# Casting k and q of the first pair inside the set-up of the decays, and loading f on the Activation queue

## The chip, the cores and the metric

The kernel runs on one core of a Trainium2 chip. The metric is the device time of one execution in microseconds (us), as the median of several runs.

## What is computed

Two blocks in a row. The first is causal attention with a forget gate over 8 batches, 8 heads, 576 positions and a head size of 64; the second mixes the sequence in the frequency domain with one 512 x 512 complex matrix for each of 64 modes. Cut to what matters:

```
scores = (q @ k.T) / 8
cum    = cumsum(log(clip(f, 1e-4, 1)))            # one row of 576 for each batch and head
attn   = softmax(causal(scores + cum[i] - cum[j]))
x      = (attn @ v), heads side by side           # 8 x 576 x 512
X      = rfft(x over the sequence)[:64 modes]
Y      = X @ (w_r + i w_i), mode by mode          # 2 x 64 x 512 x 512 weights, float32 in HBM
u      = x + irfft(Y)
out    = u + relu(u @ w_ch)
```

## The kernel before

The attention is worked through in 32 steps `s`, two for each of 16 pairs. A pair is two batches and two heads, and its two steps are the two heads. For each pair, k, q and v are loaded into staging tiles (`emit_loads`, lines 254 to 273). There are three sets of staging tiles, `STG = 3`, so pair 3 uses the tiles of pair 0 again. All loads except f and v of pair 0 are issued on the GpSimd queue (POOL in the profile) by `pool_dma`, and in the order in which they are written. Between them, on the same queue, stand the weight tiles of the modes (`emit_w_load`): each is two transfers of 512 KB into one of nine ring buffers `wb`.

`emit_transposes(pr, what)` (lines 474 to 517) brings one of k, q, v of a pair into the layout that the matmuls need. First VectorE (DVE) casts the staging tile into a tile `kb`, `qb` or `vb` (lines 482 and 486). For v this is a product with `wdec9`, a table of decays. Then TensorE (PE) transposes nine blocks in two groups of five and four (line 500), each group into one PSUM tile `tp`. Then each group is copied out: k by ScalarE (ACT) into `KT` (line 513), q by VectorE into `QTs` (line 515), v by ScalarE into `VT` (line 517). The pool `psT`, with the tag "tr", has two PSUM buffers. The set-up of the decays uses the same two buffers.

The set-up of the decays comes first. f is loaded, ScalarE takes its logarithm (line 344), VectorE sums it along the row (the scan, line 349) and makes two rearranged copies `cum2` (line 360). TensorE transposes the sums into `cum_ps` (line 353), with `ident_f`, the float32 copy of the identity (line 331), as one operand. VectorE copies them to `cumT`, TensorE broadcasts one row of that into `R_ps`, VectorE forms `biasA` and ScalarE its exponential `wdec` (line 389), of which VectorE then clears a corner (line 390). Then nine transposes of `cum2` go to two PSUM tiles `cum9_ps`, five and four (line 397); VectorE subtracts them from a constant (line 404, two instructions for each tile), and ScalarE's exponential of that is `wdec9` (line 412). Behind all this comes `emit_transposes(0, "kqv")`.

In each step the scores go through PSUM to ScalarE's exponential `E` (line 559), are masked by VectorE (line 574), and are multiplied with v (line 597). From step 9 on, matmuls of the modes (line 186) stand between them, and each mode tile that is done frees a ring buffer for the next weight load.

A scheduler orders each engine's instructions by the order in which they are written and by when it thinks that their inputs are ready. `tc.keep_in_program_order(ins)` pins an instruction behind the instruction that was written just before it for the same engine. Before the change, the casts of the first three pairs, the loads on the GpSimd queue and the three iotas of the set-up are pinned.

Of the kernel before, what the change touches and what calls it, by code (L numbers as in the profile page):

```python
# [9 lines left out]
BF16 = mybir.dt.bfloat16  # L10
I32 = mybir.dt.int32
ALU = mybir.AluOpType
# [3 lines left out]
def _strided(ap: bass.AP, free_dims, offset_elems: int = 0) -> bass.AP:  # L16
    new_ap = [list(ap.ap[0])] + [list(x) for x in free_dims]
    return bass.AP(tensor=ap.tensor, offset=ap.offset + offset_elems, ap=new_ap)
# [3 lines left out]
def kernel(  # L22
# [11 lines left out]
    nc = tc.nc  # L34
    B, H, S, Dh = q.shape
# [7 lines left out]
    NDC = D // 128  # L43
    BH = B * H
# [9 lines left out]
    RP = 64  # L54
    NR = S // RP
    RG = ((0, 5), (5, 4))
    NRING = 9
    STG = 3
# [9 lines left out]
    ident_bf = const.tile([128, 128], BF16, name="ident_bf")  # L68
    wch = const.tile([128, NDC, D], BF16, name="wch")
    bas = const.tile([128, NSB + 1, 2, NM], BF16, name="bas")  # L70
    sel = [const.tile([128, 130], BF16, name=f"sel{r}") for r in range(2)]
# [12 lines left out]
    def tile_of(n):  # L84
# [2 lines left out]
        g = (n - NTH + GL) % NTH  # L87
        return 2, g ^ 4 if GL // 2 <= g < GL else g

    def pool_dma(dst, src):  # L90
        tc.keep_in_program_order(nc.gpsimd.dma_start(dst, src))  # L91

    def wb_tile(n, *dims):
        if n != late.get("nx"):
# [111 lines left out]
    def stage(i):  # L206
        if i != 1:
            return {
                nm: stq.tile(
                    [128, 2, NR, Dh], F32 if nm == "v" else BF16, name=f"st{nm}{i}"  # L210
                )
                for nm in "kqv"
            }
        n = 2 * NR * Dh
        flat = {
            "k": wx[:, 0:n],
            "q": wx[:, n : 2 * n],
            "v": wx[:, 2 * n : 4 * n].bitcast(F32),
        }
        return {  # L220
            nm: t.rearrange("p (b r d) -> p b r d", b=2, r=NR)
            for nm, t in flat.items()
        }

    with ExitStack() as actx:
        stq = actx.enter_context(tc.tile_pool(name="stq", bufs=1))
        qkb = actx.enter_context(tc.tile_pool(name="qkb", bufs=2))
        kt = actx.enter_context(tc.tile_pool(name="kt", bufs=1))
        qtp = actx.enter_context(tc.tile_pool(name="qtp", bufs=2))
# [11 lines left out]
        psT = actx.enter_context(  # L241
            tc.tile_pool(name="psT", bufs=2, space=bass.MemoryType.PSUM)
        )
# [6 lines left out]
        wdec9 = ssb.tile([128, NR, B, NDC], BF16, name="wdec9")  # L250
        NE = 2
        QKVst = [stage(i) for i in range(STG)]
        VTs = [kt.tile([128, 2, SP], BF16, name=f"VT{i}") for i in range(2)]
        KTs = [kt.tile([128, 2, SP], BF16, name=f"KT{i}") for i in range(2)]
        Es = [epl.tile([128, 2, EW], BF16, name=f"E{i}") for i in range(NE)]

        steps = [(dc, bp, h) for dc in range(NDC) for bp in range(B // 2) for h in (0, 1)]
        NPR = len(steps) // 2

        def emit_loads(pr):  # L260
            dc, bp, _ = steps[2 * pr]
            for nm, src in (("k", k), ("q", q), ("v", v)):
# [9 lines left out]
                else:  # L272
                    pool_dma(dst, ap)

        used = [0]

        def scratch(parts, *dims):
# [11 lines left out]
        ident_f = scratch(128, 128)  # L289
        ftf = scratch(128, S)  # L290
        ft = ftf[:BH, :]
        nc.sync.dma_start(ft[:], f.rearrange("b h s -> (b h) s"))
        emit_loads(0)
        nc.gpsimd.memset(trimask[:, :], 1.0)
        nc.gpsimd.affine_select(
# [32 lines left out]
        tc.keep_in_program_order(  # L328
            nc.gpsimd.iota(m_i[:], pattern=[[1, NM]], base=0, channel_multiplier=0)
        )  # L330
        nc.vector.tensor_copy(ident_f[:, :], ident_bf[:, :])
        for r, t in enumerate(sel):
            nc.vector.memset(t[:, :], 0.0)
            nc.vector.tensor_copy(
                _strided(t[:, 1:2], [[2, 64]]), _strided(ident_bf[:, r : r + 1], [[2, 64]])
            )
        for t in VTs:
            nc.vector.memset(t[:, :, S:SP], 0.0)
        for t in KTs:
# [3 lines left out]
        lf = ft  # L343
        nc.scalar.activation(lf[:], ft[:], ACT.Ln)
        wide = scratch(128, 2 * S)
        onesS = wide[:BH, 0:S]
        nc.vector.memset(onesS[:], 1.0)
        cum = scratch(BH, S)
        nc.vector.tensor_tensor_scan(cum[:], onesS[:], lf[:], 0.0, ALU.mult, ALU.add)
        cum_ps = psT.tile([128, NSB, BH], F32, tag="tr", name="cum_ps")  # L350
        for sc in range(NSB):
            ns = SBLK[sc]
# [4 lines left out]
            )  # L357
        cum2 = wide[:BH, :].rearrange("c (r h p) -> c r h p", r=NR, h=2)
        for h in range(2):
            nc.vector.tensor_copy(  # L360
                cum2[:, :, h, :], _strided(cum[:, 0:1], [[1, NR], [NR, RP]])
            )
        cumT = scratch(128, NSB, BH)
        nc.vector.tensor_copy(cumT[:, 0:4, :], cum_ps[:, 0:4, :])
        nc.vector.tensor_copy(cumT[:64, 4, :], cum_ps[:64, 4, :])
        ones_row = scratch(1, 128)
        nc.vector.memset(ones_row[:], 1.0)
        R_ps = psT.tile([128, BH], F32, tag="tr", name="R_ps")
# [5 lines left out]
            stop=True,  # L374
        )
        Rb = ssb.tile([128, BH], F32, name="Rb")
        nc.vector.tensor_copy(Rb[:], R_ps[:])
        biasA = scratch(128, NSB, BH)
        nc.vector.tensor_tensor(
            biasA[:, 0:4, :],  # L380
            _strided(Rb[:, :], [[0, 4], [1, BH]]),
            cumT[:, 0:4, :],
            ALU.subtract,
        )
        nc.vector.tensor_tensor(
            biasA[:64, 4, :], Rb[:64, :], cumT[:64, 4, :], ALU.subtract
        )
        nc.vector.memset(biasA[64:128, 4, :], 0.0)
        nc.scalar.activation(wdec[:, :, :], biasA[:, :, :], ACT.Exp)
# [1 line left out]
        bias9 = ftf[:, 0 : NR * B * NDC].rearrange(  # L391
            "p (r b c) -> p r b c", r=NR, b=B
        )
        for r0, n in RG:
            cum9_ps = psT.tile([128, 5, BH], F32, tag="tr", name="cum9_ps")
            for r in range(r0, r0 + n):
                nc.tensor.transpose(
                    cum9_ps[:, r - r0, :],
                    cum2[:, r, :, :].rearrange("c h p -> c (h p)"),
                    ident_f[:BH, :BH],  # L400
                )
            for h in range(2):
                hs = slice(h * 64, h * 64 + 64)
                nc.vector.tensor_tensor(
                    bias9[hs, r0 : r0 + n, :, :],
                    _strided(Rb[hs, h : h + 1], [[0, n], [H, B], [2, NDC]]),
                    _strided(
                        cum9_ps[hs, 0, h : h + 1], [[BH, n], [H, B], [2, NDC]]
                    ),
                    ALU.subtract,  # L410
                )
        nc.scalar.activation(wdec9[:, :, :, :], bias9[:, :, :, :], ACT.Exp)

# [54 lines left out]
                    BI[:, sc * 128 : (sc + 1) * 128], bip[:, :], coef[:], None, ALU.mult  # L468
                )


        QT, vaugs = {}, {}

        def emit_transposes(pr, what):
            dc, bp, _ = steps[2 * pr]
            for which in what:
                st = QKVst[pr % STG][which]
                if which == "q":
                    QT[pr] = qtp.tile([128, 2, S], BF16, tag="QT", name="QTs")
                sb = qkb.tile([128, NR, 2, Dh], BF16, tag="cb", name=which + "b")  # L480
                if which != "v":
                    ins = nc.vector.tensor_copy(
                        sb[:, :, :, :].rearrange("p r b d -> p b r d"), st[:, :, :, :]
                    )
                else:
                    ins = nc.vector.tensor_tensor(
                        sb[:, :, :, :],
                        st[:, :, :, :].rearrange("p b r d -> p r b d"),
                        _strided(
                            wdec9[:, 0, 2 * bp, dc : dc + 1],  # L490
                            [[B * NDC, NR], [NDC, 2], [0, Dh]],
                        ),
                        ALU.mult,
                    )
                if pr < STG:
                    tc.keep_in_program_order(ins)
                for r0, n in RG:
                    tp = psT.tile([128, 5, 2, RP], BF16, tag="tr", name="tp")
                    for r in range(r0, r0 + n):
                        nc.tensor.transpose(  # L500
                            tp[:, r - r0, :, :].rearrange("c h p -> c (h p)"),
                            sb[:, r, :, :].rearrange("p b d -> p (b d)"),
                            ident_bf[:, :],
                        )
                    tv = tp[:, 0:n, :, :].rearrange("c r h p -> c h p r")

                    def rows(t):
                        return t.rearrange("c h (p r) -> c h p r", r=NR)[
                            :, :, :, r0 : r0 + n
                        ]  # L510

                    if which == "k":
                        nc.scalar.copy(rows(KTs[pr % 2][:, :, 0:S]), tv)  # L513
                    elif which == "q":
                        nc.vector.tensor_copy(rows(QT[pr][:, :, :]), tv)  # L515
                    else:
                        nc.scalar.copy(rows(VTs[pr % 2][:, :, 0:S]), tv)  # L517

        def emit_vback(s):
            dc, bp, h = steps[s]  # L520
# [166 lines left out]
        def next_w():  # L687
            nonlocal nload
            if nload < NDC * NG:
                emit_w_load(nload)  # L690
                nload += 1

        emit_transposes(0, "kqv")
        for s in range(NS + 1):
            pr, h = s // 2, s % 2
            if s == 0:
# [10 lines left out]
            if pr + 1 < NPR:  # L707
                emit_transposes(pr + 1, ("kq", "v")[h])
# [24 lines left out]
    with ExitStack() as bctx:  # L733
# [80 lines left out]
        with ExitStack() as cctx:  # L814
            psBig = cctx.enter_context(
                tc.tile_pool(
                    name="psBig", bufs=6, space=bass.MemoryType.PSUM, side="right"
# [79 lines left out]
            while nmode < NT - 1:  # L897
# [9 lines left out]
                if nmode > NT - GL:  # L907
                    assert nx == B
                    while done < (nmode - NT + GL) * (len(parts) - 2) // (GL - 2):
                        a, sb = parts[done]  # L910
# [4 lines left out]
            for a, sb in parts[done:]:  # L915
# [5 lines left out]
                    name=name,  # L921
# [127 lines left out]
        for b in range(2, B):  # L1049
            for t in range(2):  # L1050
# [4 lines left out]
                name="psX", bufs=1, space=bass.MemoryType.PSUM, reuse_waits="tile"  # L1055
# [56 lines left out]
```

## Time and profile before

| | |
|---|---|
| median of 7 runs | 438.2 us (436.59 to 438.82) |
| the profiled execution's own time | 438.23 us |
| its span in the profile | 436.4 us |
| busy: PE, DVE, ACT, POOL | 83%, 60%, 52%, 29% of the span |
| bytes moved by DMA | 97.37 MB, mean 223 GB/s |
| landing of f after its issue | 2.9 us |
| landing of k, q, v of pair 0 after their issue | 6.6, 7.2, 5.4 us |

The span is the part of the execution that the profile covers; 1.8 us lie around it. "Idle before" in a row of the timeline is the time in which that engine had nothing to do before the row, with what ended the wait. A releaser is inferred, so where the named one had long been done, it was another one. A row of several instructions (x2, x9) carries the time from the start of the first to the end of the last, or their busy time where there are gaps.

### The profile page before, as it was taken

How to read it: one execution, taken by the hardware profiler on the slowest of the kernel's cores; microseconds unless marked ns; L12 is line 12 of the kernel's file. 1: busy time of each engine (PE TensorE's matmuls, PEld its weight loads, DVE VectorE, ACT ScalarE, POOL GpSimd, SP SyncE). 2: the span in 40 equal slices, each digit the busy share in tenths (PEclk: the TensorE clock that was granted, in tenths of full speed). 3: DMA queues.
4: the chain of work that ended last, by engine and by line, in shares of the span. 5: the costliest groups of instructions: out<-in, count | busy, mean ns of one | idle time of the engine just before them, and what ended most of it. 6: DMA issues, size and time to landing. Idle time of an engine off the chain costs nothing.

```text
span 436.4 us, 12194 instructions
## 1 busy us (share of the span) xinstructions
PE 363.1 (83%) x5247; PEld 248.7 (57%) x5265; DVE 263.0 (60%) x658; ACT 225.5 (52%) x340; POOL 128.7 (29%) x202
## 2 busy tenths in 40 slices
PE   2697699998978879788778988699999997799881
PEld 1464466776665656556656666566665654454440
DVE  5678778877455656545556578632332665544892
ACT  3678378775526264364553727124334443633770
POOL 7333332153233232332333221233222223200600
PEclk9997889998558686656585569689999999989997
DMA  8999999999999999999999999999999999995697
GB/s 179 234 235 241 234 236 239 231 197 238 228 220 237 219 229 236 211 237 228 219 237 212 210 212 211 211 210 212 211 212 211 211 211 212 211 211 104 239 370 281
DMA packets 50693, 97.37 MB, mean 223 GB/s; under 512 B 3760, under 2 KB 12944, under 8 KB 50640
## 3 DMA queue, kind: packets, MB, share of 16 engines
q0 software_dynamic: 46688, 86.16, 100.9%
q1 hardware_dynamic: 3632, 9.91, 6.3%
q8 instruction: 41, 0.67, 0.6%
q10 hardware_dynamic: 320, 0.52, 0.5%
q14 instruction: 12, 0.10, 0.1%
HBM read 163.73 MB, written 9.44 MB: 397 GB/s over the span
## 4 chain that ended last, share of the span: by engine, by line
PE 31%; DMA 28%; ACT 12%; DVE 9%; issue 4%; POOL 1%; ACTq 0%; DVEq 0%
DMA wb<-in_moe_w_i_dram 25%; ACT E L559 8%; PE pav L597 7%; PE ps L552 6%; PE A L186 5%; PE tp L500 5%; DMA stv<-in_v_dram 3%; DVE QTs L515 2%; PE px L640 2%; ACT KT L513 2%; PE vp L524 2%; DVE XT L654 1%; ACT VT L517 1%; DVE os L984 1%; PE px L665 1%
## 5 line engine op out<-in xcount | busy, mean ns | idle before, releaser
L559 ACT ACTIVATE E<-ps 128x1024 bf16<-128x1024 f32 (+1 forms) x128 | 101.6, 852 | 28.7 <-PE ps L552 19.1
L91 POOL DMA_DIRECT2D wb<-in_moe_w_r_dram x64 | 42.6, 665 | 132.9 <-PE A L186 38.5
L186 PE MATMUL A<-XT,wb 128*128 128x16 bf16 x1984 | 69.7, 181 | 10.0 <-DMA wb<-in_moe_w_i_dram 5.3
L186 PEld LDWEIGHTS <-wb 128*128 128x128 bf16 x1984 | 63.3, 100 | 24.7 <-issue 11.8
L552 PE MATMUL ps<-QTs,KT 64*128 64x64 bf16 (+4 forms) x384 | 58.6, 329 | 15.2 <-ACT E L559 14.0
L91 POOL DMA_DIRECT2D wb<-in_moe_w_i_dram x64 | 42.3, 660 | 73.7 <-DMA wb<-in_moe_w_i_dram 33.2
L597 PE MATMUL pav<-va,E 128*128 128x65 bf16 (+1 forms) x1088 | 58.3, 216 | 4.1 <-DVE x_all L619 3.5
L597 PEld LDWEIGHTS <-E 128*128 128x128 bf16 (+1 forms) x1088 | 48.0, 119 | 19.4 <-issue 8.4
L574 DVE TENSOR_TENSOR E<-E,trimask 128x256 bf16<-128x256 bf16 (+2 forms) x128 | 37.1, 302 | 19.5 <-ACT E L559 18.9
L517 ACT COPY VT<-tp 128x640 bf16<-128x640 bf16 (+1 forms) x32 | 23.3, 755 | 33.3 <-PE tp L500 33.0
L845 ACT CAST XW<-pxw 128x512 bf16<-128x512 f32 x36 | 20.7, 587 | 35.3 <-PE pxw L838 23.4
L552 PEld LDWEIGHTS <-KT 64*128 64x128 bf16 x384 | 19.2, 100 | 30.5 <-issue 21.8
L888 ACT CAST XW<-pB 128x512 bf16<-128x512 f32 x36 | 21.0, 586 | 28.2 <-PE pB L806 21.0
L838 PE MATMUL pxw<-wch,yy 128*128 128x512 bf16 x133 | 33.3, 382 | 1.1 <-issue 0.5
L887 DVE CAST x_all<-pA 128x512 bf16<-128x512 f32 x36 | 24.9, 692 | 15.4 <-PE pA L806 14.5
L513 ACT COPY KT<-tp 128x640 bf16<-128x640 bf16 (+1 forms) x32 | 22.1, 754 | 22.2 <-PE tp L500 22.2
L515 DVE COPY QTs<-tp 128x640 bf16<-128x640 bf16 (+1 forms) x32 | 23.2, 767 | 14.3 <-PE tp L500 14.2
L619 DVE TENSOR_TENSOR x_all<-pav,rcp 128x384 bf16<-128x384 f32 x64 | 29.1, 454 | 0.8
L608 DVE RECIPROCAL rcp<-pav 128x6 f32<-128x6 f32 x64 | 12.1, 189 | 27.5 <-PE pav L597 26.6
L151 DVE TENSOR_TENSOR YTe<-A,Yacc 128x128 bf16<-128x128 f32 x16 | 5.9, 368 | 32.8 <-PE A L186 32.8
L806 PEld LDWEIGHTS <-ident_bf 64*64 64x64 bf16 (+1 forms) x300 | 14.1, 107 | 16.5 <-issue 8.4
L524 PE MATMUL vp<-ident_bf,VT 128*128 128x128 bf16 x160 | 18.2, 259 | 5.0 <-DVE QTs L515 4.2
(143 smaller groups left out, 606.0 us busy)
## 6 DMA issues: line engine op xcount, KB each, us to landing
wb<-in_moe_w_r_dram POOLq DMA_DIRECT2D x62, 512.0 KB, 16.5
wb<-in_moe_w_i_dram POOLq DMA_DIRECT2D x62, 512.0 KB, 17.1
out_dram<-os SPq DMA_DIRECT2D x12, 512.0 KB, 5.2
stv<-in_v_dram POOLq DMA_DIRECT2D x10, 576.0 KB, 15.4
stk<-in_k_dram POOLq DMA_DIRECT2D x11, 288.0 KB, 15.3
stq<-in_q_dram POOLq DMA_DIRECT2D x11, 288.0 KB, 15.3
wx<-in_v_dram POOLq DMA_DIRECT2D x5, 576.0 KB, 15.2
out_dram<-uo SPq DMA_DIRECT2D x3, 512.0 KB, 3.9
```

The lines of the kernel that those rows point to most:

```text
L91: tc.keep_in_program_order(nc.gpsimd.dma_start(dst, src))
L186: nc.tensor.matmul(A[:, eb, mi, :], lhsT=w_of(mi, eb * 128), rhs=x_of(m), start=(i == 0), stop=(i == len(terms) - 1),)
L513: nc.scalar.copy(rows(KTs[pr % 2][:, :, 0:S]), tv)
L515: nc.vector.tensor_copy(rows(QT[pr][:, :, :]), tv)
L517: nc.scalar.copy(rows(VTs[pr % 2][:, :, 0:S]), tv)
L524: nc.tensor.transpose(vp[:, sc, :, :].rearrange("p b d -> p (b d)"), VTs[s // 2 % 2][:, h, sc * 128 : (sc + 1) * 128], ident_bf[:, :],)
L552: nc.tensor.matmul(ps[:, b, o : o + n], lhsT=KTs[pr % 2][bs, h, jb * 128 : (jb + 1) * 128], rhs=QT[pr][bs, h, jb * 128 + c0 : jb * 128 + c ...
L559: nc.scalar.activation(E[:, :, piece * 512 : piece * 512 + w], ps[:, :, 0:w], ACT.Exp, scale=scale,)
L574: nc.vector.tensor_tensor(dg, dg, tr, ALU.mult)
L597: nc.tensor.matmul(pav[64 * half : 64 * half + w, slot, :], lhsT=E[:, b, c : c + (w - 1) * st + 1 : st], rhs=va[:, jb, b, :], start=(n == ...
L619: nc.vector.tensor_tensor(xo, pi, ri, ALU.mult)
L838: nc.tensor.matmul(pxw[:, :], lhsT=xT[:, eb, i * 128 : (i + 1) * 128], rhs=wch[:, eb, :], start=(eb == 0), stop=(eb == NDC - 1),)
```

## The change

- f is loaded by a DMA that ScalarE issues (the Activation queue). Before, SyncE (SP) issued it, ahead of the load of v of pair 0. That load stays on SP and is now SP's first.
- The casts and transposes of k and q of pair 0 move into the loop over the two `cum9_ps` tiles: k is cast, transposed and copied ahead of the first tile, q ahead of the second. Only v stays behind the set-up.
- VectorE's instructions of the set-up, from the scan to the subtractions, are pinned in the order in which they are written, and the copy `ident_f` is written behind the scan.
- The two tiles `sel` (a clearing and a strided copy each) are made behind `emit_transposes(0, "v")`.
- `emit_transposes` is defined further up. Its text does not change.

```diff
+    keep = tc.keep_in_program_order
 ...
-        nc.sync.dma_start(ft[:], f.rearrange("b h s -> (b h) s"))
+        nc.scalar.dma_start(ft[:], f.rearrange("b h s -> (b h) s"))
         emit_loads(0)
 ...
-        nc.vector.tensor_copy(ident_f[:, :], ident_bf[:, :])
-        for r, t in enumerate(sel):
-            nc.vector.memset(t[:, :], 0.0)
-            nc.vector.tensor_copy(
-                _strided(t[:, 1:2], [[2, 64]]), _strided(ident_bf[:, r : r + 1], [[2, 64]])
-            )
 ...
-        nc.vector.tensor_tensor_scan(cum[:], onesS[:], lf[:], 0.0, ALU.mult, ALU.add)
+        keep(
+            nc.vector.tensor_tensor_scan(
+                cum[:], onesS[:], lf[:], 0.0, ALU.mult, ALU.add
+            )
+        )
+        keep(nc.vector.tensor_copy(ident_f[:, :], ident_bf[:, :]))
 ...
         # the copies cum2, cumT and Rb, and the two instructions of biasA: each now inside keep(...)
 ...
         nc.scalar.activation(wdec[:, :, :], biasA[:, :, :], ACT.Exp)
         nc.vector.memset(wdec[64:128, 4, :], 0.0)
 ...
-        for r0, n in RG:
+        for (r0, n), which in zip(RG, "kq"):
+            emit_transposes(0, which)
             cum9_ps = psT.tile([128, 5, BH], F32, tag="tr", name="cum9_ps")
             for r in range(r0, r0 + n):
                 nc.tensor.transpose(cum9_ps[:, r - r0, :], ...)
             for h in range(2):
                 hs = slice(h * 64, h * 64 + 64)
-                nc.vector.tensor_tensor(bias9[hs, r0 : r0 + n, :, :], ...)
+                keep(nc.vector.tensor_tensor(bias9[hs, r0 : r0 + n, :, :], ...))
         nc.scalar.activation(wdec9[:, :, :, :], bias9[:, :, :, :], ACT.Exp)
 ...
-        emit_transposes(0, "kqv")
+        emit_transposes(0, "v")
+        for r, t in enumerate(sel):
+            nc.vector.memset(t[:, :], 0.0)
+            nc.vector.tensor_copy(
+                _strided(t[:, 1:2], [[2, 64]]), _strided(ident_bf[:, r : r + 1], [[2, 64]])
+            )
         for s in range(NS + 1):
```

## The prediction

> **What bounds the kernel now.** I read the page's DMA rows first, then the windows in which the transfer rate falls, then the POOL queue around them, and last the first 17 us.
>
> ```profile
> DMA  8999999999999999999999999999999999995697
> GB/s 179 234 235 241 234 236 239 231 197 238 228 220 237 219 229 236 211 237 228 219 237 212 210 212 211 211 210 212 211 212 211 211 211 212 211 211 104 239 370 281
> q0 software_dynamic: 46688, 86.16, 100.9%
> ```
>
> The loads of the POOL queue keep the 16 DMA engines busy from slice 2 (11 us) to slice 36 (about 395 us). Behind that lie some 35 us from the last weight, which TensorE receives at 401.05 us, to the end. So the time is the start of the stream, its bytes, its gaps and this tail. The change touches neither bytes nor tail; it can act through the start and the gaps. Gaps are few: the slices below 210 GB/s inside the stream are one, slice 9. The windows of 1 us show it (columns: busy time of PE, PEld, DVE, ACT, POOL, then clock, DMA share, GB/s):
>
> ```profile
> 85.00:86.00 1.00, 0.92 (x16) 0.53 (x13) 1.00 (x2) 1.00 (x3) 0.00 (x0) 1.00 1.05 179
> 89.00:90.00 1.00, 1.00 (x34) 0.96 (x34) 0.86 (x4) 0.75 (x1) 1.00 (x3) 1.00 1.10 207
> 90.00:91.00 1.00, 1.00 (x22) 0.71 (x19) 0.29 (x1) 1.00 (x2) 1.00 (x2) 1.00 1.39 174
> 91.00:92.00 1.00, 1.00 (x22) 0.80 (x20) 0.88 (x4) 0.55 (x3) 0.32 (x1) 1.00 0.86 156
> ```
>
> Against the 211 GB/s that weights reach elsewhere, 85 to 88 us lack 32, 11 and 6, and 90 to 94 us lack 37, 55, 18 and 18: 177 KB, or 0.84 us of stream. The POOL queue tells why:
>
> ```profile
> 71.04 0.76 POOL L91 DMA_DIRECT2D wch<-in_moe_w_ch_dram  x1 [0.41 <-DMA stv<-in_v_dram]
> 83.39 0.61 POOL L91 DMA_DIRECT2D wb<-in_moe_w_r_dram  x1 [11.58 <-PE vp L524]
> 87.95 0.62 POOL L91 DMA_DIRECT2D wb<-in_moe_w_r_dram  x1 [3.33 <-PE ps L552]
> ```
>
> ```profile
> wb<-in_moe_w_r_dram POOLq DMA_DIRECT2D x1, 512.0 KB, 6.7
> ```
>
> By 71 us all nine weight buffers are full, and POOL stands still until the first modes' matmuls (line 186, 82.24 us in the chain) free one. The load issued at 83.39 lands after 6.7 us (second fence), where the median is 16.5: almost nothing was queued ahead of it. So at 83 to 92 us the stream has no reserve, and when the modes come is decided by the compute since 0 us. One us later there is one us of stream lost; earlier, at most the 0.84 us come back. At 281.95, the next long wait (7.73 us), landing takes 10.1 us, so 3.4 us of reserve remain there.
>
> What sets the compute's start:
>
> ```profile
> 4.42 1.35 DVE L349 TENSOR_TENSOR_SCAN Yacc<-Yacc 64x576 f32<-64x576 f32 x1 [1.93 <-ACT Yacc L344]
> 7.07 0.25 DVE L331 CAST Yacc<-ident_bf 128x128 f32<-128x128 bf16 x1
> 9.30 1.22 PE L397 MATMUL cum_ps<-Yacc 64*128 64x64 f32 x9
> 10.14 0.64 DVE L404 TENSOR_TENSOR Yacc<-Rb,cum_ps 64x160 f32<-64x160 f32 x2
> 11.51 0.59 DVE L482 COPY kb<-stk 128x1152 bf16<-128x1152 bf16 x1
> 12.03 0.44 DVE L482 COPY qb<-stq 128x1152 bf16<-128x1152 bf16 x1
> 12.92 1.36 ACT L513 COPY KT<-tp 128x640 bf16<-128x640 bf16 x2 [0.89 <-PE tp L500]
> 14.45 1.45 DVE L515 COPY QTs<-tp 128x640 bf16<-128x640 bf16 x2 [1.88 <-PE tp L500]
> 15.80 1.34 DVE L486 TENSOR_TENSOR vb<-stv,wdec 128x1152 bf16<-128x1152 f32 x1
> 16.60 1.94 ACT L559 ACTIVATE E<-ps 128x1024 bf16<-128x1024 f32 x2 [2.33 <-PE ps L552]
> ```
>
> The second cast starts only when all of the set-up is done, though k landed at 1.34 + 6.6 = 7.9 us. But `cum9_ps` runs at 9.3 to 11.5 while its PSUM buffers have no other user.
>
> **The change part by part.**
>
> *f on the Activation queue.* SP's issues stand at 0.81 (f, 0.59 us) and 1.46 (v), so v goes 0.65 us earlier. The stream's first windows (2 to 6 us) are below its later busy share, so 0 to 0.65 us of transfer move forward; but from 71 us POOL waits for compute, so this is worth nothing at the end unless compute gains too: 0. f itself goes out at 0.81 as before, but no longer alone: the first window with data, 2 to 3 us, moves some 187 KB, more than f's 144. If v's bytes run between f's, f's 0.7 us of transfer at about 200 GB/s doubles. Bounds 0 and 0.65 us later; I take 0.4, since v starts with f but POOL's k does not. Everything behind the logarithm moves by it. ACT's issue (0.6 us) precedes a table load of 1.28 us, done at 2.7, before f is there: nothing.
>
> The Trainium skill, "DMA: Bandwidth & Descriptors", has in "Queues, rings and completion order" that each DMA engine takes turns between queues that have work, a packet at a time, and in "Issuing engines are not separate DMA queues" that another issuer saves its issue time only. That speaks against this part; by it f is 0.65 us later and the sum below 0.25 us more. No row of this trace shows f and v on two queues.
>
> *`ident_f` behind the scan.* The scan ends at 5.77. TensorE waits for `ident_f` (7.07 to 7.32; its first transpose is at 7.37). Cast at 5.8, it lets the transposes run beside the two `cum2` copies (1.34 us), and `cumT` follows at 7.35, not 8.21. The two `sel` copies (0.30 us) leave the path as well; later they lie in VectorE's idle time (6.5 of 10 us busy at 10 to 20 us; without that cover they cost their 0.30). `Rb`, `biasA`, the exponential and the clearing of `wdec` (10.78) follow as before, 0.85 us earlier; with f, 0.45. The clearing ends at 10.4.
>
> *k.* kb is pinned behind that clearing: 10.4, not 11.51. With the old distances (0.65 to TensorE, 1.41 to the copies) `KT` runs 11.8 to 13.2, against 12.92 to 14.28.
>
> *The first `cum9_ps` behind k.* It is written behind k's two groups, so its turn in the two "tr" buffers comes when `KT`'s first half is out, 12.5. Line 404 followed its transposes by 0.84: 13.35 to 14.0. Should the scheduler give it a buffer ahead of k, this wait falls away (a rival below).
>
> *q.* qb is pinned behind those subtractions: 14.0, not 12.03. With 0.44 for the cast, 0.05 to TensorE and 0.73 to `QTs` it stands at 15.2 to 16.7, against 14.45 to 15.90: 0.8 later. So k's gain does not reach the scores, which need both.
>
> *The second `cum9_ps` and v.* Its buffer comes free with the first half of `QTs`, 15.95; its subtractions are pinned behind `QTs`: 16.7 to 17.3; the exponential (0.44) now stands at 17.3 to 17.8 on ACT, where at 11.58 it hid in idle time. vb waits for it: 17.8, not 15.80, 2.0 later. Queued behind it on VectorE are the casts of pair 1 and the masks; PE's transposes of v wait too.
>
> *The first E* (scores 0.05 and E 0.65 after q) would be at 17.4, and behind the moved exponential at 17.8: 1.2 later than 16.60. Between 16.6 and 28.8 ACT waits 0.15, 0.80 and 1.14 us, and from 28.8 to 41.5 it runs without a gap. So the delay there lies between nothing (2.1 us of waits take it) and v's 2.0. I take E's 1.2: the waits belong to transposes that v delays more than E, so they are no reserve. From 46 to 82 the chain of waits goes from engine to engine without slack, to the modes, and the stream loses 1.2 us.
>
> Sum: 438.23 + 1.2 = 439.4 us. The profiled execution's own time is the median 438.2 within 0.03.
>
> **The rivals.**
>
> *The buffers go the other way, and it is faster.* If the scheduler transposes `cum9_ps` while k is being cast, line 404 follows kb at 11.0, qb stands at 11.6, `QTs` ends at about 14.7, 1.2 before now, and v is about where it was. For it: TensorE is idle from 10.5 to 12.16. Against it: the buffers are shared in the order in which they are written wherever the trace lets me see it. Then the modes come earlier, and the stream gets back at most its 0.84 us, plus 0.1 to 0.2 of v's earlier start: 437.2.
>
> *The delay is absorbed.* If E's and v's lateness goes into ACT's 2.1 us of waits, the modes come on time: 438.2, within 0.5 either way.
>
> *f is issued behind the table load.* If ACT loads its table first (1.28 us, at 0.81), f lands 1.3 us later, all of it on the path: 438.23 + 1.2 + 1.3 less 0.4 (v is then past) = 440.3.
>
> **How the numbers follow.** The forecast has 0.40, f behind the table load 0.08, absorbed 0.28, the faster one 0.24. A measurement of this kernel tells 0.2%, 0.9 us, from no change. So slower has 0.48, within 0.28, faster 0.24. The forecast's own range is 438.9 (f not delayed, some waits taken) to 440.2 (v's 2.0 in full). The range reaches from the faster case, 437.1, to the table load with half a us more, 440.8.
>
> **What would show it.** Right: `QTs` ends near 16.7, line 412 stands near 17.3, vb near 17.8, the first E past 17; the first mode tile is later than 82.24, and windows between 84 and 93 us fall below 150 GB/s. It is wrong if line 397's first five run before k's transposes, if POOL's long wait ends before 83 us, or if those windows stay near 200.

## The result and the profile after

The changed kernel takes 440.05 us in the median (438.53 to 441.31) against 438.13 us for the kernel before: 1.0046 times as long, with a 95% interval of 1.0033 to 1.0060. By the ratio that is 2.0 us slower. The forecast was 439.4 us, slower; the measured time lies inside its range of 437.1 to 440.8.

The profiled execution of the changed kernel took 440.04 us, its span 438.0 us. Its page, in the rows that were shown of before:

```profile
DMA  9999999999999999999999999999999999994697
GB/s 180 234 236 243 231 235 238 204 205 238 223 225 237 214 235 236 212 236 229 219 237 211 211 212 211 211 211 211 212 211 211 211 211 211 211 211 90 237 371 279
q0 software_dynamic: 46688, 86.16, 100.6%
```

The bytes are the same. The dip is now in slices 8 and 9 (204 and 205 GB/s). Its windows of 1 us, with the same columns as before:

```profile
85.00:86.00 1.00, 1.00 (x17) 0.65 (x14) 0.88 (x5) 0.52 (x2) 0.42 (x1) 1.00 0.65 113
86.00:87.00 1.00, 1.00 (x12) 0.50 (x11) 0.72 (x3) 0.44 (x1) 0.81 (x2) 1.00 0.60 56
87.00:88.00 1.00, 0.95 (x20) 0.85 (x20) 0.21 (x1) 1.00 (x2) 0.00 (x0) 1.00 0.66 84
```

The rate falls to half and then to a quarter of its 211 GB/s: the DMA engines now stand still for part of this time (share 0.60 to 0.66, where the windows from 88 to 93 us show 1.1 to 1.2). The three windows lack 380 KB, or 1.8 us, against 0.84 us in all the gaps of before. The POOL queue again gives the reason, and the landing of the load that ends the long wait stands in the second fence:

```profile
70.96 0.76 POOL L93 DMA_DIRECT2D wch<-in_moe_w_ch_dram  x1 [0.41 <-DMA stv<-in_v_dram]
85.58 0.61 POOL L93 DMA_DIRECT2D wb<-in_moe_w_r_dram  x1 [13.87 <-PE pav L607]
90.67 0.61 POOL L93 DMA_DIRECT2D wb<-in_moe_w_r_dram  x1 [3.86 <-PE ps L562]
```

```profile
wb<-in_moe_w_r_dram POOLq DMA_DIRECT2D x1, 512.0 KB, 5.1
```

POOL's last load before the wait goes out when it did (70.96 against 71.04), but the first mode tile frees a buffer 2.2 us later (85.58 against 83.39), and the load then lands after 5.1 us: the queue is empty. The timeline of the start shows where the lateness begins:

```profile
5.39 0.68 ACT L387 ACTIVATE Yacc<-Yacc 64x576 f32<-64x576 f32 x1 [2.71 <-DMA Yacc<-in_f_dram]
11.76 0.46 DVE L287 COPY kb<-stk 128x1152 bf16<-128x1152 bf16 x1
13.02 1.36 ACT L318 COPY KT<-tp 128x640 bf16<-128x640 bf16 x2 [1.45 <-PE tp L305]
13.83 0.79 PE L452 MATMUL cum_ps<-Yacc 64*128 64x64 f32 x5 [0.42 <-ACT KT L318]
14.66 0.65 DVE L460 TENSOR_TENSOR Yacc<-Rb,cum_ps 64x160 f32<-64x160 f32 x2 [2.34 <-PE cum_ps L452]
15.34 0.46 DVE L287 COPY qb<-stq 128x1152 bf16<-128x1152 bf16 x1
16.61 1.46 DVE L320 COPY QTs<-tp 128x640 bf16<-128x640 bf16 x2 [0.81 <-PE tp L305]
18.90 0.44 ACT L469 ACTIVATE wdec<-Yacc 128x288 bf16<-128x288 f32 x1 [4.51 <-DVE Yacc L460]
19.25 2.83 ACT L569 ACTIVATE E<-ps 128x1024 bf16<-128x1024 f32 x3
19.37 1.36 DVE L291 TENSOR_TENSOR vb<-stv,wdec 128x1152 bf16<-128x1152 f32 x1 [0.57 <-ACT wdec L469]
```

Two things are to be seen. The logarithm starts at 5.39, not at 3.71 as in the kernel before, and what it waited for is the load of f (the row of before first, then the two issues of the changed kernel):

```profile
3.71 0.68 ACT L344 ACTIVATE Yacc<-Yacc 64x576 f32<-64x576 f32 x1 [1.62 <-DMA Yacc<-in_f_dram]
0.81 0.45 SPq L273 DMA_DIRECT2D stv<-in_v_dram  x1
0.81 0.56 ACTq L341 DMA_DIRECT2D Yacc<-in_f_dram  x1
```

And from the cast of k on, the order is the new one: the first `cum9_ps` transposes (13.83) wait for `KT`'s copy, the cast of q comes behind their subtractions, and the exponential `wdec9` stands just ahead of the first E. The first E is 2.65 us later than before, vb 3.57 us.

In the trace's packets, v's 272 on SP's queue start between 1.93 and 4.13 us, f's 80 on the Activation queue between 3.81 and 4.49. Both transfers were issued at 0.81 us. f waited until v was nearly done. Each of the two transfers has 16 packets of 4 bytes; v's start between 3.80 and 4.13 us, late in it. The first of them starts at 3.804 us and f's first packet at 3.810, the second at 3.826 and f's second packet at 3.832. So f seems to follow v on one DMA engine after the other, with an engine's whole share of v moved before it begins f. The trace does not name the engine of a packet, so this is a reading.

To follow the stream, I took from each trace the time at which the POOL queue's packets had moved 17, 20 and 83 MB. The changed kernel stands 0.14 us ahead of before at 17 MB (78.4 us), 1.12 behind at 20 MB (93.4 us), and 0.76 behind at 83 MB (384 us). So the stream falls behind between 78 and 93 us and is still behind 290 us later.

### The profile page after: what moved, and what is told of

It reads as the page before. It is cut to its first block, busy times and chain, and to the rows that moved or that the text cites. A ratio compares the mean times of both kernels' runs of the same rounds, so it can differ in the third digit from the quotient of the medians.

```text
span 438.0 us, 12194 instructions
## 1 busy us (share of the span) xinstructions
PE 356.5 (81%) x5247; PEld 243.1 (56%) x5265; DVE 263.1 (60%) x658; ACT 224.5 (51%) x340; POOL 129.0 (29%) x202
## 4 chain that ended last, share of the span: by engine, by line
DMA 40%; PE 33%; ACT 11%; DVE 8%; issue 5%; DVEq 0%; ACTq 0%; POOL 0%
DMA wb<-in_moe_w_i_dram 39%; ACT E L569 7%; PE ps L562 7%; PE pav L607 7%; PE tp L305 6%; PE A L188 5%; ACT KT L318 2%; DVE QTs L320 2%; PE pz L821 2%; PE vp L534 2%; PE px L650 1%; PE pu L821 1%; PE px L675 1%; DVE os L999 1%; ACT VT L322 1%
## 5 line engine op out<-in xcount | busy, mean ns | idle before, releaser
L562 PE MATMUL ps<-QTs,KT 64*128 64x64 bf16 (+4 forms) x384 | 57.7, 317 | 20.4 <-ACT E L569 20.1
L607 PE MATMUL pav<-va,E 128*128 128x65 bf16 (+1 forms) x1088 | 53.9, 206 | 3.5 <-DVE x_all L629 3.1
L607 PEld LDWEIGHTS <-E 128*128 128x128 bf16 (+1 forms) x1088 | 44.2, 112 | 19.1 <-issue 9.3
L305 PE MATMUL tp<-ident_bf,qb 128*128 128x128 bf16 x144 | 17.3, 278 | 5.3 <-ACT KT L318 3.9
```

Source lines behind the costliest of these rows:

```text
L305: nc.tensor.transpose(tp[:, r - r0, :, :].rearrange("c h p -> c (h p)"), sb[:, r, :, :].rearrange("p b d -> p (b d)"), ident_bf[:, :],)
L562: nc.tensor.matmul(ps[:, b, o : o + n], lhsT=KTs[pr % 2][bs, h, jb * 128 : (jb + 1) * 128], rhs=QT[pr][bs, h, jb * 128 + c0 : jb * 128 + c ...
L607: nc.tensor.matmul(pav[64 * half : 64 * half + w, slot, :], lhsT=E[:, b, c : c + (w - 1) * st + 1 : st], rhs=va[:, jb, b, :], start=(n == ...
```

## The experiments

The question after the result was not whether the start is late, but which half of the change makes it late, f or the order, and whether lateness at 83 us is the cause at all. Each ratio is against executions of the kernel before that were measured with it. A difference in us is that ratio times 438 us; it can lie up to 0.7 us from the difference of the medians.

In the expectations, the times of single packets are counted from a zero that lies 0.31 us ahead of the timeline's. So the 1.64 to 1.69 us and 1.39 to 1.42 us from issue to first packet in e9's are 1.33 to 1.38 and 1.08 to 1.12. The times of instructions and the distances between packets are right.

**f back on SP ahead of v (e1): the order alone.** The changed kernel with

```diff
-        nc.scalar.dma_start(ft[:], f.rearrange("b h s -> (b h) s"))
+        nc.sync.dma_start(ft[:], f.rearrange("b h s -> (b h) s"))
```

> The changed kernel with f back on SP ahead of v, so that only the new order of the set-up is left. In the changed profile the logarithm started at 5.39 us, 1.68 later than before, and every later step of the first pair was late by that and by the new order. Theory: the two add. Then here the logarithm starts at 3.7, the cast of k at 10.1, the cast of q at 13.7, QTs at 15.0, the first E at 17.6 (before 16.60), POOL's long wait ends 0.4 to 0.9 us later than the 83.39 of before, and the time is 438.4 to 439.0. Rival: the late f is the whole loss, and the order alone costs nothing or gains: first E no later than 16.7, time 437.5 to 438.2.

Measured: 1.0008 of before (0.9995 to 1.0022), 0.35 us with an interval of -0.2 to 1.0. The steps came as expected, as the timeline of its profile shows:

```profile
10.01 0.46 DVE L287 COPY kb<-stk 128x1152 bf16<-128x1152 bf16 x1
13.60 0.46 DVE L287 COPY qb<-stq 128x1152 bf16<-128x1152 bf16 x1
14.87 1.45 DVE L320 COPY QTs<-tp 128x640 bf16<-128x640 bf16 x2 [0.81 <-PE tp L305]
17.50 2.83 ACT L569 ACTIVATE E<-ps 128x1024 bf16<-128x1024 f32 x3
```

k is cast 1.5 us earlier than before and yet the first E is 0.9 us later. Of that 0.9 us the time shows little, but its interval holds all of it too. The profile's wait at POOL ended at 84.83, 1.4 us later than before, where 0.4 to 0.9 was expected; the stream was 0.39 us behind at 20 MB and 0.06 at 83 MB. The median, 438.28, lies between the rival's range and the theory's, so this run does not decide whether the order alone costs anything.

**f on the Activation queue, and nothing else (e2, and again as e7).** The kernel before with the opposite edit:

```diff
-        nc.sync.dma_start(ft[:], f.rearrange("b h s -> (b h) s"))
+        nc.scalar.dma_start(ft[:], f.rearrange("b h s -> (b h) s"))
```

> The kernel before with nothing changed but f on the Activation queue, v of pair 0 first on SP. Theory (the two parts add): the logarithm starts at 5.4, the cast of k at 12.9 to 13.2, the first E at 18.0 to 18.3, POOL's long wait ends at 84.5 to 85.0, and the stream loses that: 439.0 to 439.8. Rival (the order is the whole loss, lateness of f is absorbed before the modes): POOL's wait ends at 83.4 and the time is that of before within 0.5.

Measured: 1.0038 (1.0020 to 1.0055), 1.7 us slower. So f's part carries most of the loss, and the two parts add up: 0.0038 + 0.0008 = 0.0046. That they meet to the last digit is chance, as the intervals reach 0.0018 and 0.0014 to either side. The logarithm started at 5.58 and the first E at 18.29, close to what was expected. But in this profile POOL's wait ended at 83.16, no later than before, and the stream was 0.4 us ahead: a miss. The execution that was profiled was the fastest of twelve (437.63 us), so the kernel was measured and profiled a second time.

> The kernel with f's part alone once more. Its first profile fell on its fastest execution of 12 (437.63 against a median of 439.64), with POOL's long wait over at 83.16 although the first E stood at 18.29. Theory: the granted clock between 35 and 60 us differs from execution to execution and moves the modes by a us or more; with the usual clock the wait ends at 84.3 to 85.5 here, the stream is 0.5 to 1.7 us behind before's at 20 MB, and the median is again 439.0 to 440. Rival: 1.7 us at the first E never reach the modes; the wait ends at 83.5 or earlier again, and the median's lateness comes from the tail.

Measured: 1.0041 (1.0019 to 1.0062). The wait ended at 84.55 and the stream was 0.68 us behind at 20 MB, as the theory had it; the median, 440.12, is just over the range given. The two profiles differ in the clock granted to TensorE between 55 and 60 us, 1.00 in the first and 0.69 in the second (between 50 and 55 us it is the other way round, 0.67 and 0.84). The other profiles point the same way. Over all fourteen, the time from the first E to the end of POOL's wait is the shorter the higher the clock of 55 to 60 us is (correlation -0.80; with the mean clock of 35 to 60 us only -0.34). In e4, e1 and e9, whose first E stand within 0.15 us, clocks of 1.00, 0.66 and 0.50 go with waits that end at 83.15, 84.83 and 85.19. No run sets the clock, so that it made the difference is likely, and not shown.

**Why f came late: one queue for both (e4), the queues exchanged (e3), v a little later (e9).**

```diff
 # e4: v behind f on the Activation queue, nothing on SP
                 if nm == "v" and pr < 1:
-                    nc.sync.dma_start(dst, ap)
+                    nc.scalar.dma_start(dst, ap)
 # e3: the same edit, and f on SP (the edit of e1)
 # e9: the changed kernel, with a small load ahead of v on SP
+        tiny = ssb.tile([1, 64], F32, name="tiny")
+        nc.sync.dma_start(tiny[:, :], f[0, 0:1, 0:64])
         emit_loads(0)
```

> The changed kernel with v of pair 0 on the Activation queue too, behind f, so that SP loads nothing at the start. Theory A, f waited behind v's packets of the other queue: here nothing stands ahead of f, its packets move from 2.2 to 2.6 us on and the logarithm starts at 3.6 to 3.9. Theory B, the Activation queue is slow to start (its first packet in the changed kernel moved at 4.1): the logarithm starts at 5.2 to 5.5 here too. By A the first E is at about 17.6 and the time 438.4 to 439.0, by B as in the changed kernel, 440.

Measured: 1.0007 (0.9990 to 1.0025); the median, 437.93, is half a us under the range given. The logarithm started at 3.81. The Activation queue is not slow to start; f's first packet moved at 2.14, against 2.19 on SP in the kernel before.

> The changed kernel with the two queues of f and v exchanged: f on SP, v of pair 0 on the Activation queue, both still issued at 0.81. Theory A1, of two transfers issued together SP's goes first: f's packets move from 2.4 us on, the logarithm starts at 3.6 to 4.0, and the time is that of the kernel with f on SP ahead of v, 438.0 to 438.8. Theory A2, the larger transfer, or whichever is ready first, goes ahead whatever its queue: the logarithm starts at 5 to 5.6 and the time is near 440. Sharing by turns, as the prediction had it: 4.0 to 4.4.

Measured: 1.0065 (1.0039 to 1.0090). With f on SP and v on the Activation queue, f is late again: v's packets start at 1.89, f's at 3.67, and the logarithm at 5.67, against 5 to 5.6 expected. It is not a matter of which queue f is on.

> The changed kernel (f on the Activation queue, v of pair 0 on SP) with a transfer of 256 bytes from f, into a tile that nothing reads, issued on SP ahead of v, so that v is issued about 0.5 us later. In the swap f came last on SP as it had on the Activation queue; alone or in front, f's first packet moved 1.64 to 1.69 us after its issue, v's 1.39 to 1.42. Theory, whichever transfer's packets start first is served to its end: v's would now start at 2.7, f's at 2.4 to 2.5, the logarithm starts at 3.6 to 4.0, the first E at 17.4 to 17.8, and the time is that of the kernel with f on SP ahead of v, 0 to 1.2 us over before. Rival, v goes first whenever both are queued: the logarithm starts at 5.4 to 6 and the time is 1.5 to 2.5 us over before.

Measured: 1.0007 (0.9989 to 1.0026). The small load takes SP's first issue, v goes out behind it, and f's packets move from 2.15 to 2.86 us. Now v's follow f's last ones (2.64 us). The logarithm is back, in the timeline of its profile:

```profile
3.59 0.68 ACT L389 ACTIVATE Yacc<-Yacc 64x576 f32<-64x576 f32 x1 [0.93 <-DMA Yacc<-in_f_dram]
17.42 2.83 ACT L571 ACTIVATE E<-ps 128x1024 bf16<-128x1024 f32 x3
```

SP issues v at 1.22 there, so 0.4 us between the issues of f and v decide over 1.8 us in f. Issued together, v's first packet moves about 0.2 us before f's would (1.89 to 1.93 in the changed kernel, e2 and e3, against 2.14 in e4), and f is then served behind it. More than half of these 0.2 us can stand in the issues: in these kernels v's takes 0.43 to 0.45 us and f's 0.55 to 0.59, whichever engine issues it. Why f's takes longer is open. The execution that was profiled was the slowest of twelve (441.38 us), which may be why its POOL wait ended as late as 85.19; it is the ratio that shows the loss gone.

**The order's own wait: another PSUM buffer (e5, and again as e10).** The kernel of e1 with `cum9_ps` in the one buffer of the attention output, which is first used at 25.6 us in the kernel before:

```diff
-            cum9_ps = psT.tile([128, 5, BH], F32, tag="tr", name="cum9_ps")
+            cum9_ps = psO.tile([128, 5, BH], F32, tag="av", name="cum9_ps")
```

> The changed kernel with f back on SP ahead of v, and with the two cum9_ps tiles in the PSUM buffer of the attention output (one buffer, idle until 25 us) and not in the two that the transposes of k and q use. Theory, the first cum9_ps waits for KT's copy and holds back the cast of q: that wait goes, the subtractions follow the cast of k at 10.7, the cast of q starts at 11.3 to 11.8, QTs at 13.6 to 14.0, the first E at 15.5 to 16.0, 0.6 to 1.1 before the 16.60 of before; POOL's long wait ends 0.5 to 1 us earlier, and the time is 437.3 to 437.9, at most 0.84 us below before. Rival, the pinned order on VectorE holds q back whatever the buffer: the cast of q stays at 13.5 or later and the time is that of the kernel with f on SP.

Measured: 0.9989 (0.9974 to 1.0004); the medians are equal within 0.04 us. The cast of q starts 1.05 us behind k's, where it was 3.59 us in e1, and everything behind it is about 2 us earlier than in e1 (timeline of its first profile):

```profile
10.21 0.46 DVE L287 COPY kb<-stk 128x1152 bf16<-128x1152 bf16 x1
11.26 0.60 DVE L287 COPY qb<-stq 128x1152 bf16<-128x1152 bf16 x1
13.17 1.45 DVE L320 COPY QTs<-tp 128x640 bf16<-128x640 bf16 x2 [1.21 <-PE tp L305]
15.53 2.83 ACT L569 ACTIVATE E<-ps 128x1024 bf16<-128x1024 f32 x3
```

The second measurement of the same kernel:

> The kernel with cum9_ps in a PSUM buffer of its own and f on SP ahead of v once more, for its interval: it was 0.9989 of before, 0.9974 to 1.0004. In its profile the stream had no gap left and was 1.0 to 1.3 us ahead of before's. Theory: 0.4 to 1.1 us under before. Rival: the stream's gain is lost in the tail (36.9 us there, against 35.4) in every execution, and the time is that of before within 0.3.

Measured: 0.9984 (0.9971 to 0.9998), 0.7 us under before. POOL's wait ended at 80.60, the windows between 84 and 93 us carry 201 to 221 GB/s, and the stream is 0.9 us ahead at 20 MB. This is the version that the experiments point to. It beats the changed kernel clearly (the intervals of e5 and e10 end below those of the changed kernel and e6); its lead over the kernel before is at the edge of what can be told (see e12).

**`ident_f` alone (e11).** The kernel before with the scan, `ident_f` behind it and the two `cum2` copies pinned, and the `sel` tiles made behind pair 0:

```diff
-        nc.vector.tensor_copy(ident_f[:, :], ident_bf[:, :])
 ...
+        tc.keep_in_program_order(nc.vector.tensor_tensor_scan(...))
+        tc.keep_in_program_order(nc.vector.tensor_copy(ident_f[:, :], ident_bf[:, :]))
+        # and tc.keep_in_program_order(...) round each of the two cum2 copies
```

> The kernel before with one piece of the change alone: ident_f cast straight behind the scan and pinned there with the scan and the two cum2 copies, and the sel tiles made behind the transposes of pair 0; f on SP ahead of v, and k and q of pair 0 cast behind the set-up as before. Theory: TensorE's transposes of the sums run beside the cum2 copies, everything from cumT on is 0.6 to 0.9 us earlier, the first E at 15.7 to 16.0, POOL's long wait ends 0.5 to 1 us earlier, and the time is 0.3 to 0.9 us under before, since the stream has 0.84 us of gaps to close. Rival: the cast of k waits for the loads, and the first E stays at 16.5; the time is that of before.

Measured: 0.9995 (0.9980 to 1.0010). The steps come as expected or a little earlier: k is cast at 10.66 and the first E stands at 15.61, 1.0 us earlier; POOL's wait ends at 81.81, 1.6 us earlier, and the stream is 1.0 us ahead at 20 MB. The time is not told apart from before, where 0.3 to 0.9 us less was expected.

**More lateness (e8).** The kernel before with

```diff
+        for _ in range(5):
+            nc.scalar.copy(ft[:], ft[:])
         nc.scalar.activation(lf[:], ft[:], ACT.Ln)
```

> The kernel before with ScalarE copying f onto itself five times ahead of the logarithm (0.68 us each, nothing else changed), a lateness of 2.9 to 3.4 us at the logarithm and no change of any transfer or order. Theory (each us by which the modes come late is a us of stream): the first E at 19.6 to 20.0, POOL's long wait over at 85.5 to 87, the stream 2 to 3 us behind, the time 2.0 to 3.4 us over before. Rival (what costs is where f and v stand on the queues, not lateness): within 0.7 us of before.

Measured, over five executions: 1.0082 (1.0045 to 1.0119), 3.6 us slower, without touching a transfer. The copies took 0.70 us each. Behind them, at 7.02 us, stands the table load of 1.28 us that before was over at 2.1 us, ahead of f. So the lateness was 4.6 us at the logarithm, more than meant. POOL's wait ended 4.8 us later, and the stream was 3.7 us behind at 20 MB and 3.8 at 83 MB:

```profile
88.22 0.62 POOL L91 DMA_DIRECT2D wb<-in_moe_w_r_dram  x1 [17.09 <-PE vp L526]
```

**Second profiles of the changed kernel (e6) and of before (e12).**

> The changed kernel once more, for a second profile of it, since one profile holds one execution's clock. In the first profile the stream had fallen 1.1 us behind that of before at 20 MB (about 93 us), kept 0.8 of that to its end, and the tail behind the last weight took 36.9 us where the other profiles had 34.9 to 35.4, with matmuls at half clock just behind 401 us. Theory (the loss is made at 80 to 95 us): the stream is again 0.5 to 2 us behind at 20 MB and the logarithm again starts at 5.2 to 5.6. Rival (the loss is made in the tail): the stream is at most 0.3 us behind and the tail again takes over 36.5 us.

Measured: 1.0050 (1.0027 to 1.0074). The logarithm started at 5.93 (5.2 to 5.6 was expected), the wait ended at 86.14, the stream was 1.67 us behind at 20 MB and 1.43 at 83 MB. The tail behind the last weight took 35.6 us, not 36.9: the rival falls.

> The kernel before once more, unchanged, for a second profile: how far do two executions of the same kernel differ in the steps that were compared? The first E should stand at 16.5 to 16.8 again, since TensorE's clock is full until then. If the granted clock between 35 and 60 us moves the modes by itself, POOL's long wait ends anywhere from 82 to 84.5 and the stream at 20 MB is up to 1 us to either side of the first profile. If it ends at 83.3 to 83.5 again, the scatter seen among the other kernels (83.16 and 84.55 for the same one) is their own. Half clock just behind 400 us, seen in both profiles of the changed kernel, would show here that it is not the change's doing. Time: 0.998 to 1.002 of before.

Measured: 1.0017 (1.0003 to 1.0032) for the same program. The first E stood at 16.46, the wait ended at 83.57, the stream was within 0.2 us of the first profile's, and there was no half clock behind 400 us. So the steps repeat well, while the interval of a kernel against itself just misses 1. A difference of 0.2% is therefore not settled by one comparison here, and that holds for e10's gain.

All profiles together, in the order of POOL's wait (stream at 20 MB against the first profile of before, negative is ahead):

| kernel | first E | POOL's wait ends | stream, us | time, ratio |
|---|---|---|---|---|
| e10, own buffer | 15.52 | 80.60 | -0.88 | 0.9984 |
| e11, `ident_f` alone | 15.61 | 81.81 | -1.04 | 0.9995 |
| e5, own buffer | 15.53 | 81.88 | -0.97 | 0.9989 |
| e4, one queue | 17.57 | 83.15 | -0.65 | 1.0007 |
| e2, f part | 18.29 | 83.16 | -0.38 | 1.0038 |
| before | 16.60 | 83.39 | 0 | 1 |
| e12, before | 16.46 | 83.57 | -0.13 | 1.0017 |
| e7, f part | 18.45 | 84.55 | 0.68 | 1.0041 |
| e1, order | 17.50 | 84.83 | 0.39 | 1.0008 |
| e9, v later | 17.42 | 85.19 | 0.85 | 1.0007 |
| changed | 19.25 | 85.58 | 1.12 | 1.0046 |
| e3, swap | 19.43 | 85.86 | 1.39 | 1.0065 |
| e6, changed | 19.69 | 86.14 | 1.67 | 1.0050 |
| e8, late start | 21.17 | 88.22 | 3.68 | 1.0082 |

Before 82 us a microsecond at POOL is worth nothing to the stream: three profiles stand at about -1.0, whether the wait ends at 80.6 or 81.9. Behind 84 us it is worth a microsecond: from e1 to e8, 3.4 us of wait cost 3.3 us of stream. Between the two it is worth less: in the changed kernel the wait ended 2.2 us later than before, and the stream lost 1.1. The ratios rest on 5 to 13 executions of each kernel; the other columns are of one execution each, and in it the end of the wait moves against the first E by up to 1.5 us either way (e1, e4 and e9 have the same first E and waits that end at 83.15 to 85.19).

A straight line through the columns of the first E and of the time, an estimate from these fourteen rows, gives 0.73 us of time for each microsecond by which the first E is late. The rows lie within 0.7 us of it.

## Why the prediction was right, and what was mis-sized in it

**The bound and the direction held.** The claim that the time hangs on when the first modes free a buffer is shown by e8, where lateness alone costs 3.6 us, and by the table. That each microsecond of it is a whole microsecond of time was too simple: the line through the table gives 0.73. The limit on the other side held: the two kernels that start a microsecond earlier (e5 with e10, and e11) are 0.9 to 1.0 us ahead at 20 MB. Of this they have 0.3 us already at 17 MB, ahead of the gaps, as e8 has, so the gaps gave back 0.6 to 0.7 of the 0.84 us. (The 0.1 to 0.2 us for v's earlier start have no place here, since f stands ahead of v in these kernels.) At 83 MB they are 1.3 to 1.4 us ahead; where the further 0.4 us come from was not followed.

**The order's steps held one by one.** In e1, where f is prompt, the forecast's times less its 0.4 us for f are 10.0 for kb, 13.6 for qb, 14.8 for `QTs`, 17.4 for vb and 17.4 for the first E. Measured: 10.01, 13.60, 14.87, 17.63 and 17.50. That the first `cum9_ps` waits for `KT`'s copy, argued against the rival in which it goes ahead, is shown by the row at 13.83 and by e5, where another buffer takes 2.0 us off the first E.

**The order's price is not settled.** Of 0.8 us (the first E's 1.2 less f's 0.4), the time shows 0.35 us, between -0.2 and 1.0, an interval that holds both 0.8 and nothing. e4 and e9, in which f is prompt too, read 0.3 us each. The argument that ACT's waits are no reserve is neither shown nor refuted.

**The step that was mis-sized is f.** The forecast took 0.4 us with bounds of 0 and 0.65, on the ground that v's bytes would run between f's. f came 1.7 us late, outside those bounds, since the two did not share: f's packets stood behind v's. In the changed kernel every step from the end of `QTs` to vb comes 1.4 to 1.6 us later than forecast, and these 1.3 us are most of that. In time this term is 1.7 us (e2: 0.9 to 2.4), not 0.4. The upper bound should have been v's whole transfer, 1.9 to 2.5 us (590 KB at the 308 to 233 GB/s of the windows of before from 3 to 5 us), since nothing in the trace of before showed how two queues share. The forecast's sum was 1.2 us, the change measures 2.0 (1.4 to 2.6). The sum that the runs give is 1.7 + 0.35 = 2.05 us: f was too small by 1.3 us, and the order perhaps too large by 0.45, which then hid part of the error. That is luck, and so is it that the forecast's own range holds the result: its upper end, 440.2, was put there for v's lateness.

The Trainium skill, "DMA: Bandwidth & Descriptors", "Queues, rings and completion order", says that each engine takes turns between queues a packet at a time, where a packet is typically some 9 to 17 descriptors. The prediction read this as v's bytes running between f's. The traces show no such turns: in three kernels with both issued at 0.81 us, f's packets began when v's were nearly done. By the page's count that is no contradiction if the 17 packets of the trace that v has for each engine (an estimate, 272 spread evenly over 16) are one packet of the page; no run here tests it. The same page's "Issuing engines are not separate DMA queues" says that DMAs run on the same 16 engines, whichever engine started them, and interleave. e4 and e3 agree with the first: which engine issues f makes no difference. The second these two transfers do not show.

**The rivals.** f behind the table load did not happen: the Activation queue issued f at 0.81, and the table load began at 1.40. But its price came true for another reason: it had f 1.3 us later than the forecast did, all of it on the path, for 440.3, and f came 1.3 us later than forecast, behind v. Whether the order's part alone is absorbed (nothing) or costs the forecast's 0.8 us, its 0.35 us do not decide. The faster case, buffers shared the other way, is what e5 had to build.

**What stays open.** The two profiles of the changed kernel show the stream 0.8 and 1.4 us behind at 83 MB, while the time differs by 2.0 and 2.2 us. The stretch from 83 MB to the last weight's matmuls took between 17.4 and 19.7 us in all these profiles, so one profile can't place the rest. In the first profile of the changed kernel, matmuls behind 401 us ran at half clock and the tail took 36.9 us; that is not the change's doing, since e6 lacks that tail and e5 has it.

## What to carry to other kernels

Where a saturated stream of loads stands still once for compute to free a buffer, look at how soon the next load lands: 6.7 us against a usual 16.5 says that little reserve is left, and then lateness in the set-up, 80 us earlier, comes back in the whole time: 3.6 of 4.6 us in e8, some 0.73 for each microsecond over all kernels here. A microsecond gained is worth at most the gap that there is.

A small transfer that heads a chain of dependent work should be issued clearly ahead of a large one, and not beside it on another queue: 0.4 us between the issues decided over 1.8 us. And moving a cast forward pays only if everything that shares its PSUM buffers can move with it; here k gained 1.5 us and q lost 1.6.

## What the runs showed of the hardware that was not expected

Two transfers issued at the same time on SP's and the Activation queue were served one behind the other: v (272 packets, 1.9 to 4.2 us) first, f (80 packets, 3.6 to 4.8 us) after it, on whichever queue each stood. f's first packet started 6 ns behind the first of v's sixteen 4-byte packets in all five profiles of these kernels. With v's issue 0.4 us later, f was done at 2.9 us, and v followed it.

The same program can have its first modes 1.4 us apart in two executions (e2 and e7) with the same set-up to within 0.2 us. The clock granted to TensorE between 55 and 60 us was 1.00 in the one and 0.69 in the other.
